# Moved transfers and weight splits around layer one of a fused attention and two-MLP kernel

## The chip, the cores and the metric

One core of a Trainium2 chip. The time is device microseconds of one execution. Engines: PE is TensorE (PEld its weight loads), DVE is VectorE, ACT is ScalarE, POOL is GpSimd, SP is SyncE, which here only issues DMAs. Each engine works off one queue in order.

## The reference, cut to what matters

```python
attn_out = _attn_ref(q, k, v, f)          # causal attention with decay, 4 x 8 heads, 576 x 64
x = attn_out.transpose(0, 2, 1, 3).reshape(2304, 512)
h = x @ moe_w_in; x = (h - tanh(h)) @ moe_w_out              # first MLP, 512 -> 2048 -> 512
h = x @ moe2_w_in; out = (maximum(h, 0) ** 2) @ moe2_w_out   # second MLP
```

The weights reach the kernel as float64: it reads each word as a pair of 32-bit integers and decodes it to float32 itself. All else is float32. The change concerns the second MLP only. "Layer one" below is its first matrix product, "layer two" its second.

## The kernel before, in words

Products are made in float32 accuracy: each operand is split into a high and a low part (fp32r), and each product is three matmuls (high x high, low x high, high x low). The second MLP also uses Strassen-like sums: per tile pair seven products instead of eight, so each weight pair needs seven 256-column pieces: four sums and three plain ones.

**Layer one** (`layer1`, L1185) has 24 units: three token blocks times eight weight pairs p. A step s of the code makes the first four products (6, 1, 7, 5) of unit s and the last three (2, 4, 3) of unit s - 1. Each product (`l1_product`, L1128) is six matmuls of 128x384, and advances a clock (`cw.step`) on which later work is put by a number of products: `cw.later(k, fn)` calls fn k products on. `after1` (L1145) takes a product out of PSUM with ScalarE or VectorE (L1150, L1157, L1167, L1171, L1176) into g tiles, of which there are two buffers for each half of a unit; `store1` (L1179) squares g on GpSimd (L1182) and stores it to DRAM (`gscr`, L1183).

**Weights of layer two** are prepared during layer one. For each of eight pairs: `load_w` (L146) loads the raw words in two halves (L139) into one buffer. `decode_w` (L176) decodes them half by half: ScalarE (`first`, L193 and L194) and VectorE (`bits`, L200 and L202), into `wfull`; the raw buffer serves as scratch for the second half and is free after its L202. `combine` (L232) makes the four sums on GpSimd (L244, into `wsum`) and stores sums (L247) and plain pieces (L249, L250) to a DRAM buffer `wscr`, since layer one's weights still hold the room. `wfull` and `wsum` live in two buffers called `wide`. Decodes follow each other: `decoded()` lets the next begin. In the code `load_w(2, k)` is called at the start of step 4 + 2k and `decode_w(2, k)` at step 5 + 2k (PRE = 5).

When the last token block is through with a weight pair, `final_load` (L307) loads the seven pieces of layer two's pair p from `wscr` into one of two staging buffers (L310), and `final_split` splits them (`split_all`, L287: ScalarE L294 for the high part, VectorE L295 for the low) into the room of layer one's weights. `FREED` (L1225) says at which step of the last block: the load at FREED[p] - 1, the split at FREED[p] + 1.

**Layer two** (`layer2`, L1313) has 36 blocks n. `g_load` (L1232) loads a block of g from `gscr` in four DMAs (L1241), `g_sums` makes three sums on VectorE (L1247, L1248, L1250), `g_split` (L1252) splits it on ScalarE (L1256) and VectorE (L1257) into `gc`, and `l2_product` (L1259) makes seven products of six matmuls of 128x256 (L1270), 42 per block. Block n uses pairs 2q and 2q + 1 with q = n mod 4, so the fourth block is the first to want pairs 6 and 7. Blocks 0 and 1 are loaded during layer one; the rest use buffers `gx` of a pool m3, which is opened over the room of layer one's pool m2 (staging buffers `xl`, g tiles `gt`, split y tiles `T1` to `T7`) when layer one's code ends.

**Order.** The framework puts instructions into each engine's queue by when it reckons their inputs ready, and by the code's order among those that are; `high_priority` moves an instruction forward among these. The order is fixed when the kernel is built, and an engine whose next instruction is not ready waits.

Of the kernel before, what the change touches and what calls it, by code (L numbers as in the profile page):

```python
# [109 lines left out]
def fused_kernel(ctx: ExitStack, tc: tile.TileContext, q, k, v, f, w1i, w1o, w2i, w2o, out):  # L110
# [65 lines left out]
    def decode_w(phase, fc):  # L176
# [20 lines left out]
        def bits(x):  # L197
            lo_, hi_ = spots[x]
            dst = full[:, x * w : (x + 1) * w]
            nc.vector.scalar_tensor_tensor(lo_, in0=hi_, scalar=3, in1=lo_,  # L200
                                           op0=ALU.logical_shift_left, op1=ALU.bitwise_or)
            nc.vector.scalar_tensor_tensor(dst, in0=hi_, scalar=0x80000000, in1=lo_,  # L202
                                           op0=ALU.bitwise_and, op1=ALU.bitwise_or)
            if x == 0:
                first(1)
            else:
                cw.later(LAG['wparts'], (lambda: parts(0)) if phase == 0 else (lambda: combine(phase, fc, full)))

        def parts(x):
# [22 lines left out]
    def combine(phase, p, full):  # L232
        full = full.bitcast(F32)
        (q11, q12), (q21, q22) = quarters(full, phase)
        sums = wide(f"wsum_{phase}_{p}", F32)
        s = [sums[:, 256 * x : 256 * x + 256].rearrange("p (c f) -> p c f", c=2) for x in range(4)]
        if phase == 1:
            ops = ((s[0], q21, q22, ALU.add), (s[1], s[0], q11, ALU.subtract), (s[2], q11, q21, ALU.subtract),
                   (s[3], q12, s[1], ALU.subtract))
        else:  # L240
            ops = ((s[0], q12, q11, ALU.subtract), (s[1], q22, s[0], ALU.subtract), (s[2], q12, q22, ALU.subtract),
                   (s[3], q21, s[1], ALU.subtract))
        for o, a, b, op in ops:
            nc.gpsimd.tensor_tensor(o, in0=a, in1=b, op=op)  # L244
        if phase == 2:
            w = wscr[p]
            nc.sync.dma_start(w[:, 0:4], sums.rearrange("p (k f) -> p k f", k=4))  # L247
            f4 = full.rearrange("p (k f) -> p k f", k=4)
            nc.sync.dma_start(w[:, 4:5], f4[:, 0:1])  # L249
            nc.sync.dma_start(w[:, 5:7], f4[:, 2:4])  # L250
            decoded()
            return
        v = full.rearrange("p (c f) -> p c f", c=ND)
        s4 = sums.rearrange("p (k f) -> p k f", k=4)
        work = split_plan(1, p, (v[:, :, 0:P], v[:, 2:4, P : 2 * P]), [s4[:, 0:2], s4[:, 2:4]])
        split_all(1, p, work, 1)
# [48 lines left out]
    stagew = {}  # L305

    def final_load(p):  # L307
        t = box2["m2"].tile([P, 7, 256], F32, tag="xl", name=f"wst_{p}", bufs=2)
        stagew[p] = t
        nc.sync.dma_start(t, wscr[p])  # L310

    def final_split(p):
        t = stagew.pop(p)
        split_all(2, p, split_plan(2, p, (t[:, 5:7], t[:, 4:5]), [t[:, 0:4]]), 1)

    WHERE = {1: {5: 0, 6: 1, 7: 2, 3: 3, 1: 4, 2: 5, 4: 6}, 2: {5: 0, 6: 1, 7: 2, 4: 3, 2: 4, 3: 5, 1: 6}}

# [861 lines left out]
    def store1(u, fi):  # L1179
        i, p = units1[u]  # L1180
        g = gf.pop((u, fi))
        nc.gpsimd.tensor_tensor(g, in0=g, in1=g, op=ALU.mult)  # L1182
        nc.sync.dma_start(gscr[i][:, :, 2 * p + fi], g.rearrange("p b t n -> p b (t n)"))  # L1183

    def layer1():  # L1185
        n = len(units1)
        last = n - NP2
        for s in range(n + 1):
# [10 lines left out]
                    goal = NF + p + FEED2  # L1199
            if s >= PRE and (s - PRE) % 2 == 0 and (s - PRE) // 2 < NP2:  # L1200
                decode_w(2, (s - PRE) // 2)
            if s >= PRE - 1 and (s - PRE + 1) % 2 == 0 and (s - PRE + 1) // 2 < NP2:
                load_w(2, (s - PRE + 1) // 2)
            if s == n - 3:
                g_load(0)
                g_load(1)
# [9 lines left out]
                cw.step(lambda: l1_product(*x))  # L1216
                feed.pace(goal)
            for p in range(NP2):
                if s == last + FREED[p] - 1:
                    final_load(p)  # L1220
                if s == last + FREED[p] + 1:
                    final_split(p)

    PRE = 5
    FREED = (1, 2, 3, 3, 5, 6, 7, 7)  # L1225
    AT2 = {1: (0, 0), 6: (0, 256), 7: (1, 0), 2: (1, 256), 5: (2, 0), 4: (2, 256), 3: (3, 0)}
    ORDER2 = (1, 6, 7, 2, 5, 4, 3)
    GWHERE = {7: 0, 5: 1, 6: 2, 3: 3, 1: 4, 2: 5, 4: 6}
    graws, gc, r2 = {}, {}, {}
    NG = NBLK * 4  # L1230

    def g_load(n):  # L1232
        j, q = divmod(n, 4)
        if n < 2:
            t = wp.tile([P, 8, 2, P], F32, tag=f"w{15 - n}", name=f"graw_{n}", bufs=1)
        else:
            t = box2["m3"].tile([P, 8, 2, P], F32, tag="gx", name=f"graw_{n}", bufs=2)
        graws[n] = t
        src = gscr[j // 3][:, j % 3, 4 * q : 4 * q + 4].rearrange("p (e i) (h t) -> p i h e t", i=2, h=2)
        for slot, h, i in ((0, 1, 0), (5, 0, 0), (7, 1, 1), (6, 0, 1)):  # L1240
            nc.sync.dma_start(t[:, slot], src[:, i, h])  # L1241

    def g_sums(n):
# [5 lines left out]
                                in0=t[:, 0:2].rearrange("p k e t -> p k (e t)"), in1=both, op=ALU.add)  # L1249
        nc.vector.tensor_tensor(t[:, 4], in0=t[:, 6], in1=t[:, 3], op=ALU.subtract)  # L1250

    def g_split(n):  # L1252
        t = graws.pop(n)
        c = box2["m3"].tile([P, 2, 7, 2, P], F32R, tag="gc", name=f"gc_{n}", bufs=3)
        gc[n] = c
        nc.scalar.activation(c[:, 0], t[:, 1:8], AF.Copy)  # L1256
        nc.vector.tensor_tensor(c[:, 1], in0=t[:, 1:8], in1=c[:, 0].bitcast(F32), op=ALU.subtract)  # L1257

# [54 lines left out]
    def layer2():  # L1313
        m2ctx.close()
        box2["m3"] = ctx.enter_context(tc.tile_pool(name="m3", bufs=1, reuse_waits="tile"))
        with tc.high_priority(offset=L2HOT):
            g_split(0)
        with tc.high_priority(offset=L2HOT // 2):
            g_split(1)
            for n in (2, 3):  # L1320
                g_load(n)
        for n in range(NG):
            for x, k in enumerate(ORDER2):
                if x == 1 and n + 2 < NG:
# [99 lines left out]
```

## Time and profile before

| | us |
|---|---|
| median of three runs (1072.89 to 1077.76) | 1073.69 |
| the profiled execution | 1074.4 |
| its span, first to last instruction | 1072.7 |
| TensorE busy in the span | 1014.9 |
| mean granted TensorE clock | 0.985 of full |

A row of a timeline gives the start, the duration of the merged instructions, the engine, the code line, what it writes and reads, how many, and in square brackets how long the engine stood idle before it and what ended that. Rows of SP are issues of DMAs; their data land later. Matmuls overlap, so that the duration of one is longer than its share of the time.

### The profile page before, as it was taken

Reading aid. Unit: us, or ns where it says so; the run is one execution under the profiler, and the core shown is the slowest. Engines: PE = TensorE matmul, PEld = TensorE weight load, DVE = VectorE, ACT = ScalarE, POOL = GpSimd, SP = SyncE. Lnnn points to the kernel's source line nnn. Section 1 sums busy time; section 2 is a strip of 40 time slices with the busy share of each in tenths; the row PEclk is TensorE's granted clock in tenths of the full one; section 3 lists DMA queues with packets and bytes.
Section 4 is the critical chain, followed back from the end, with each engine's and each line's share of the span. In section 5 each row is a group of like instructions: output and inputs, shape, how many; then the busy total and the mean of one; then the engine's idle time right before and its main releaser. Section 6 shows DMA issues by size and latency. Waiting matters only on the chain. (4 is left out here: it accounts for less than half of the span.)

```text
span 1072.7 us, 20563 instructions
## 1 busy us (share of the span) xinstructions
PE 1014.9 (95%) x7246; PEld 963.7 (90%) x7246; DVE 755.3 (70%) x1596; ACT 587.0 (55%) x1176; POOL 435.5 (41%) x576
## 2 busy tenths in 40 slices
PE   7989999999999999999999999988788869999997
PEld 5779899999999999999998878988688869999997
DVE  5897954777776777777755785766565877778775
ACT  5887854666766666666644664534344553233332
POOL 4763622465455654556411333655655440000000
PEclk9998999999999999999999999999999989999999
DMA  8947642433432333432131235566557763444442
GB/s 228 273 138 236 185 119 72 106 86 80 129 86 70 105 99 90 116 79 73 49 90 59 83 114 169 189 207 210 197 193 236 254 219 110 138 119 137 122 117 79
DMA packets 190903, 146.47 MB, mean 137 GB/s; under 512 B 83568, under 2 KB 168880, under 8 KB 190800
## 3 DMA queue, kind: packets, MB, share of 16 engines
q1 hardware_dynamic: 190752, 145.12, 45.7%
q8 instruction: 57, 0.93, 0.4%
q14 instruction: 46, 0.38, 0.1%
q10 hardware_dynamic: 48, 0.03, 0.0%
HBM read 100.47 MB, written 39.92 MB: 131 GB/s over the span
## 5 line engine op out<-in xcount | busy, mean ns | idle before, releaser
L970 PE MATMUL y<-ghl,w 128*128 128x256 f32 (+1 forms) x1536 | 249.1, 305 | 3.1 <-DVE ghl L951 2.0
L970 PEld LDWEIGHTS y<-ghl,w 128*128 128x128 f32 x1536 | 212.7, 192 | 16.0 <-DVE ghl L951 3.1
L930 PE MATMUL h<-x,w 128*128 128x256 f32 x1344 | 199.8, 290 | 4.9 <-POOL w L216 3.8
L930 PEld LDWEIGHTS h<-x,w 128*128 128x128 f32 x1344 | 174.5, 191 | 9.7 <-POOL w L216 5.0
L1256 ACT ACTIVATE gc<-graw 128x1792 fp32r<-128x1792 f32 x36 | 60.5, 1699 | 117.4 <-DVE graw L1250 107.1
L1138 PE MATMUL r<-yt,ws 128*128 128x384 f32 x576 | 111.0, 340 | 12.9 <-DVE g L1150 12.8
L1138 PEld LDWEIGHTS r<-yt,ws 128*128 128x128 f32 x576 | 100.9, 190 | 18.2 <-DVE g L1150 13.6
L1270 PE MATMUL o<-ws,gc 128*128 128x256 f32 x864 | 117.0, 285 | 0.0
L1270 PEld LDWEIGHTS o<-ws,gc 128*128 128x128 f32 x864 | 110.4, 194 | 0.0
L507 POOL TENSOR_SCALAR Pb<-neg,ccol 128x384 f32<-128x384 f32 (+2 forms) x96 | 69.0, 719 | 91.5 <-PE pt L714 74.0
L621 ACT ACTIVATE Pb<-Pb,st 128x384 f32<-128x384 f32 (+2 forms) x96 | 67.8, 706 | 68.2 <-DVE st L612 68.0
L1182 POOL TENSOR_TENSOR g<-g 128x768 f32<-128x768 f32 x48 | 80.3, 1683 | 54.2 <-ACT g L1171 36.3
L1270 PE MATMUL o<-wq,gc 128*128 128x256 f32 x648 | 92.3, 287 | 10.5 <-ACT gc L1256 8.4
L635 POOL TENSOR_SCALAR Pb<-Pb,st 128x384 f32<-128x384 f32 (+2 forms) x96 | 67.0, 698 | 82.0 <-DVE st L631 49.0
L1138 PE MATMUL r<-yt,wq 128*128 128x384 f32 x432 | 86.6, 343 | 11.9 <-ACT g L1167 9.0
L1270 PEld LDWEIGHTS o<-wq,gc 128*128 128x128 f32 x648 | 84.7, 195 | 11.5 <-ACT gc L1256 8.7
L1138 PEld LDWEIGHTS r<-yt,wq 128*128 128x128 f32 x432 | 76.8, 192 | 15.2 <-ACT g L1167 10.6
L1257 DVE TENSOR_TENSOR gc<-graw,gc 128x1792 fp32r<-128x1792 f32 x36 | 72.1, 2024 | 21.6 <-ACT gc L1256 21.4
L612 DVE CUSTOM_DVE_ANT_0 Pb<-s,Pb 64x288 f32<-64x288 f32 (+2 forms) x160 | 73.9, 476 | 13.6 <-PE s L677 6.9
L943 DVE TENSOR_TENSOR g<-h,g 128x512 f32<-128x512 f32 x72 | 49.5, 687 | 32.7 <-ACT g L940 31.4
L720 DVE TENSOR_TENSOR PT<-pt,PT 128x384 fp32r<-128x384 f32 (+2 forms) x96 | 55.1, 574 | 10.3 <-ACT PT L719 5.6
L951 DVE TENSOR_TENSOR ghl<-g,ghl 128x512 fp32r<-128x512 f32 x72 | 53.8, 747 | 10.2 <-ACT ghl L947 9.9
(148 smaller groups left out, 1874.7 us busy)
## 6 DMA issues: line engine op xcount, KB each, us to landing
gscr<-g SPq DMA_DIRECT2D x48, 384.0 KB, 3.4
graw<-gscr SPq DMA_DIRECT2D x144, 128.0 KB, 2.6
wraw<-in_moe_w_in_dram SPq DMA_DIRECT2D x32, 512.0 KB, 4.6
wraw<-in_moe_w_out_dram SPq DMA_DIRECT2D x32, 512.0 KB, 5.5
neg<-cscr SPq DMA_DIRECT2D x32, 288.0 KB, 3.7
wst<-wscr SPq DMA_DIRECT2D x8, 896.0 KB, 5.4
qk<-in_k_dram SPq DMA_DIRECT2D x48, 128.0 KB, 2.8
v<-in_v_dram SPq DMA_DIRECT2D x48, 128.0 KB, 2.7
```

What stands on the lines that cost most here:

```text
L507: nc.gpsimd.tensor_scalar(pb[:rows, o : o + w], t[:rows, :w], ccol[:rows, ti, b * H + h : b * H + h + 1], 1.0, op0=ALU.add, op1=ALU.mult)
L612: nc.vector.tensor_tensor_reduce(out=d, in0=t[:rows, src : src + m], in1=d, scale=-0.125, scalar=3.0e38 if j == 0 else stat(0, x)[:rows], ...
L621: nc.scalar.activation(d, d, AF.Exp, bias=stat(len(parts) - 1, x)[:rows], scale=-1.0, accum_out=stat(2, x)[:rows])
L635: nc.gpsimd.tensor_scalar(d, d, r, 1.0, op0=ALU.mult, op1=ALU.mult)
L720: cw.later(LAG['trlo'], lambda: nc.vector.tensor_tensor(dst[1], src, dst[0].bitcast(F32), op=ALU.subtract))
L930: nc.tensor.matmul(o, lhsT=win(fc, wh, dc), rhs=xpart(j, dc, xh), start=dc == 0 and wh + xh == 0, stop=dc == ND - 1 and wh == 1)
L970: nc.tensor.matmul(o, lhsT=wout(fc, wh, i * P, P), rhs=ghl[:, xh, fj * n : fj * n + n], start=s == 0 and fj == 0 and wh + xh == 0 and i % ...
L1138: nc.tensor.matmul(t, lhsT=wprod(1, p, k, wh)[:, dc * P : (dc + 1) * P], rhs=yt[i, k][:, xh, dc], start=k in FIRST and dc == 0 and wh + xh ...
L1182: nc.gpsimd.tensor_tensor(g, in0=g, in1=g, op=ALU.mult)
L1256: nc.scalar.activation(c[:, 0], t[:, 1:8], AF.Copy)
L1257: nc.vector.tensor_tensor(c[:, 1], in0=t[:, 1:8], in1=c[:, 0].bitcast(F32), op=ALU.subtract)
L1270: nc.tensor.matmul(o, lhsT=gc[n][:, gh, GWHERE[k], e], rhs=wprod(2, 2 * q + e, k, wh), start=q == 0 and e == 0 and gh + wh == 0 and c0 == ...
```

## The change

1. `bits`: after the last decode step of pair fc of layer two, `load_w(2, fc + 1)` is put one product later. In `layer1` only the first pair is still loaded by step number.
2. `combine`: the two plain stores are put one product later, the store of the sums and `decoded()` five.
3. `store1`: the store of g is put two products later; its squaring stays.
4. `final_load`: pair 6 goes to two tiles of a tag `g` (unused in layer one) and one of m3, pair 7 to the two `wide` buffers, in two DMAs; pairs 0 to 5 as before, at step FREED[p] with a new FREED. Pair 7 is loaded at the step of pair 5, pair 6 at the start of `layer2`.
5. The splits of pairs 6 and 7 are put 2 and 9 products into layer two.
6. `layer2`: the tiles of m3 are allocated in a set order (two `gx`, `st`, a pad, then `gc2`, `gc0`, `gc1` with a tag each), so that `gx` lies over the staging buffers, `gc0` over T6, T1 and T7, and `gc1` over T7, T5 and T3. `g_split(1)` comes behind the loads of blocks 2 and 3.

```diff
--- before.py
+++ after.py
@@ -204,6 +204,8 @@
             if x == 0:
                 first(1)
             else:
+                if phase == 2 and fc + 1 < NP2:
+                    cw.later(1, lambda: load_w(2, fc + 1))
                 cw.later(LAG['wparts'], (lambda: parts(0)) if phase == 0 else (lambda: combine(phase, fc, full)))
 
         def parts(x):
@@ -244,11 +246,17 @@
             nc.gpsimd.tensor_tensor(o, in0=a, in1=b, op=op)
         if phase == 2:
             w = wscr[p]
-            nc.sync.dma_start(w[:, 0:4], sums.rearrange("p (k f) -> p k f", k=4))
             f4 = full.rearrange("p (k f) -> p k f", k=4)
-            nc.sync.dma_start(w[:, 4:5], f4[:, 0:1])
-            nc.sync.dma_start(w[:, 5:7], f4[:, 2:4])
-            decoded()
+
+            def plain():
+                nc.sync.dma_start(w[:, 4:5], f4[:, 0:1])
+                nc.sync.dma_start(w[:, 5:7], f4[:, 2:4])
+
+            def summed():
+                nc.sync.dma_start(w[:, 0:4], sums.rearrange("p (k f) -> p k f", k=4))
+                decoded()
+            cw.later(1, plain)
+            cw.later(5, summed)
             return
         v = full.rearrange("p (c f) -> p c f", c=ND)
         s4 = sums.rearrange("p (k f) -> p k f", k=4)
@@ -305,13 +313,28 @@
     stagew = {}
 
     def final_load(p):
-        t = box2["m2"].tile([P, 7, 256], F32, tag="xl", name=f"wst_{p}", bufs=2)
-        stagew[p] = t
-        nc.sync.dma_start(t, wscr[p])
+        if p == NP2 - 1:
+            s_, r = wide(f"wst_s{p}", F32), wide(f"wst_r{p}", F32)[:, :768]
+            parts = [(s_, 0, 4), (r, 4, 7)]
+        elif p == NP2 - 2:
+            parts = [(m1.tile([P, 512], F32, tag="g", name=f"wst_{x}_{p}", bufs=3), x, x + 2) for x in (0, 2)]
+            r = box2["m3"].tile([P, 3 * 256], F32, tag="st", name=f"wst_r{p}", bufs=1)
+            parts.append((r, 4, 7))
+        else:
+            t = box2["m2"].tile([P, 7 * 256], F32, tag="xl", name=f"wst_{p}", bufs=2)
+            parts = [(t, 0, 7)]
+        views = []
+        for t, a, b in parts:
+            v = t.rearrange("p (k f) -> p k f", f=256)
+            nc.sync.dma_start(v, wscr[p][:, a:b])
+            views.append(v)
+        if len(views) == 1:
+            views = [views[0][:, 0:4], views[0][:, 4:7]]
+        stagew[p] = views
 
     def final_split(p):
-        t = stagew.pop(p)
-        split_all(2, p, split_plan(2, p, (t[:, 5:7], t[:, 4:5]), [t[:, 0:4]]), 1)
+        *s_, r = stagew.pop(p)
+        split_all(2, p, split_plan(2, p, (r[:, 1:3], r[:, 0:1]), s_), 1)
 
     WHERE = {1: {5: 0, 6: 1, 7: 2, 3: 3, 1: 4, 2: 5, 4: 6}, 2: {5: 0, 6: 1, 7: 2, 4: 3, 2: 4, 3: 5, 1: 6}}
 
@@ -1180,7 +1203,7 @@
         i, p = units1[u]
         g = gf.pop((u, fi))
         nc.gpsimd.tensor_tensor(g, in0=g, in1=g, op=ALU.mult)
-        nc.sync.dma_start(gscr[i][:, :, 2 * p + fi], g.rearrange("p b t n -> p b (t n)"))
+        cw.later(2, lambda: nc.sync.dma_start(gscr[i][:, :, 2 * p + fi], g.rearrange("p b t n -> p b (t n)")))
 
     def layer1():
         n = len(units1)
@@ -1199,8 +1222,8 @@
                     goal = NF + p + FEED2
             if s >= PRE and (s - PRE) % 2 == 0 and (s - PRE) // 2 < NP2:
                 decode_w(2, (s - PRE) // 2)
-            if s >= PRE - 1 and (s - PRE + 1) % 2 == 0 and (s - PRE + 1) // 2 < NP2:
-                load_w(2, (s - PRE + 1) // 2)
+            if s == PRE - 1:
+                load_w(2, 0)
             if s == n - 3:
                 g_load(0)
                 g_load(1)
@@ -1216,26 +1239,32 @@
                 cw.step(lambda: l1_product(*x))
                 feed.pace(goal)
             for p in range(NP2):
-                if s == last + FREED[p] - 1:
+                if FREED[p] is None:
+                    continue
+                if s == last + FREED[p]:
                     final_load(p)
-                if s == last + FREED[p] + 1:
+                if s == last + FREED[p] + 1 and p < NP2 - 2:
                     final_split(p)
 
     PRE = 5
-    FREED = (1, 2, 3, 3, 5, 6, 7, 7)
+    FREED = (1, 2, 3, 4, 5, 6, None, 6)
     AT2 = {1: (0, 0), 6: (0, 256), 7: (1, 0), 2: (1, 256), 5: (2, 0), 4: (2, 256), 3: (3, 0)}
     ORDER2 = (1, 6, 7, 2, 5, 4, 3)
     GWHERE = {7: 0, 5: 1, 6: 2, 3: 3, 1: 4, 2: 5, 4: 6}
     graws, gc, r2 = {}, {}, {}
     NG = NBLK * 4
 
-    def g_load(n):
-        j, q = divmod(n, 4)
+    def g_tile(n):
         if n < 2:
             t = wp.tile([P, 8, 2, P], F32, tag=f"w{15 - n}", name=f"graw_{n}", bufs=1)
         else:
             t = box2["m3"].tile([P, 8, 2, P], F32, tag="gx", name=f"graw_{n}", bufs=2)
         graws[n] = t
+        return t
+
+    def g_load(n):
+        j, q = divmod(n, 4)
+        t = graws[n] if n in graws else g_tile(n)
         src = gscr[j // 3][:, j % 3, 4 * q : 4 * q + 4].rearrange("p (e i) (h t) -> p i h e t", i=2, h=2)
         for slot, h, i in ((0, 1, 0), (5, 0, 0), (7, 1, 1), (6, 0, 1)):
             nc.sync.dma_start(t[:, slot], src[:, i, h])
@@ -1249,10 +1278,13 @@
                                 in0=t[:, 0:2].rearrange("p k e t -> p k (e t)"), in1=both, op=ALU.add)
         nc.vector.tensor_tensor(t[:, 4], in0=t[:, 6], in1=t[:, 3], op=ALU.subtract)
 
+    def gc_tile(n):
+        gc[n] = box2["m3"].tile([P, 2, 7, 2, P], F32R, tag=f"gc{n % 3}", name=f"gc_{n}", bufs=1)
+        return gc[n]
+
     def g_split(n):
         t = graws.pop(n)
-        c = box2["m3"].tile([P, 2, 7, 2, P], F32R, tag="gc", name=f"gc_{n}", bufs=3)
-        gc[n] = c
+        c = gc[n] if n in gc else gc_tile(n)
         nc.scalar.activation(c[:, 0], t[:, 1:8], AF.Copy)
         nc.vector.tensor_tensor(c[:, 1], in0=t[:, 1:8], in1=c[:, 0].bitcast(F32), op=ALU.subtract)
 
@@ -1313,12 +1345,21 @@
     def layer2():
         m2ctx.close()
         box2["m3"] = ctx.enter_context(tc.tile_pool(name="m3", bufs=1, reuse_waits="tile"))
+        for x in range(2):
+            g_tile(2 + x)
+        with tc.high_priority(offset=L2HOT):
+            final_load(NP2 - 2)
+        box2["m3"].tile([P, 256], F32, tag="pad", name="pad", bufs=1)
+        for n in (2, 0, 1):
+            gc_tile(n)
         with tc.high_priority(offset=L2HOT):
             g_split(0)
         with tc.high_priority(offset=L2HOT // 2):
-            g_split(1)
             for n in (2, 3):
                 g_load(n)
+            g_split(1)
+        cw.later(2, lambda: final_split(NP2 - 2))
+        cw.later(9, lambda: final_split(NP2 - 1))
         for n in range(NG):
             for x, k in enumerate(ORDER2):
                 if x == 1 and n + 2 < NG:
```

## Rows read from the trace of the kernel before

**Rows 1.** Table by stretches: busy us (instructions) of each engine, granted clock, DMA share, GB/s.
```profile
700.00:818.00 118.00, 98.28 (x522) 92.51 (x522) 73.39 (x105) 51.96 (x91) 71.56 (x57) 0.97 0.62 202
...
870.00:890.00 20.00, 10.95 (x58) 10.36 (x59) 15.38 (x20) 10.71 (x14) 7.64 (x4) 0.74 0.56 177
890.00:910.00 20.00, 20.00 (x169) 20.00 (x168) 16.68 (x24) 7.16 (x5) 0.00 (x0) 1.00 0.44 132
```

**Rows 2.** The chain that ended last, 844 to 880 us: start, us, what.
```profile
844.46 16.95 PE r L1138 x96
```

**Rows 3.** ScalarE's waits, 700 to 818 us: us in total, times, longest.
```profile
ACT wfull L193 <- DMA wraw<-in_moe_w_out_dram: 19.1, 4, 5.5
ACT wraw L193 <- DMA wraw<-in_moe_w_out_dram: 6.8, 2, 4.3
ACT wfull L193 <- issue: 4.9, 1, 4.9
```

**Rows 4.** Timeline of SyncE's queue, 764 to 772 us.
```profile
765.19 0.33 SPq L250 DMA_DIRECT2D wscr<-wfull  x1
767.45 0.33 SPq L247 DMA_DIRECT2D wscr<-wsum  x1
767.88 0.37 SPq L139 DMA_DIRECT2D wraw<-in_moe_w_out_dram  x1
...
770.87 0.62 SPq L139 DMA_DIRECT2D wraw<-in_moe_w_out_dram  x1
```

**Rows 5.** Timeline of all engines, 764 to 775 us.
```profile
764.47 0.69 DVE L202 SCALAR_TENSOR_TENSOR wfull<-wraw 128x512 uint32<-128x512 uint32 x1
...
772.85 0.66 ACT L193 ACTIVATE wfull<-wraw 128x512 uint32<-128x512 uint32 x1 [4.88 <-issue]
...
773.96 0.48 ACT L1167 ACTIVATE g<-r 128x384 f32<-128x384 f32 x1
...
774.49 3.51 PE L1138 MATMUL r<-yt,wq 128*128 128x384 f32 x12 [2.86 <-ACT g L1167]
```

**Rows 6.** Timeline of all engines at the boundary, 871 to 882 us.
```profile
871.84 1.21 PE L1138 MATMUL r<-yt,ws 128*128 128x384 f32 x6
...
879.68 3.29 ACT L1256 ACTIVATE gc<-graw 128x1792 fp32r<-128x1792 f32 x2 [2.83 <-DVE wq L295]
...
881.43 0.80 PE L1270 MATMUL o<-wq,gc 128*128 128x256 f32 x2 [8.39 <-ACT gc L1256]
```

**Rows 7.** Timelines of VectorE and SyncE: the freeing and the load, first and last.
```profile
699.57 0.69 DVE L202 SCALAR_TENSOR_TENSOR wfull<-wraw 128x512 uint32<-128x512 uint32 x1
...
702.97 0.37 SPq L139 DMA_DIRECT2D wraw<-in_moe_w_out_dram  x1
...
779.38 1.84 DVE L202 SCALAR_TENSOR_TENSOR wfull<-wraw 128x512 uint32<-128x512 uint32 x1
...
784.43 1.42 SPq L139 DMA_DIRECT2D wraw<-in_moe_w_out_dram  x2
```

**Rows 8.** DMA issues, 655 to 885 us: count, KB each, median us to landing.
```profile
wraw<-in_moe_w_out_dram SPq DMA_DIRECT2D x16, 512.0 KB, 5.2
...
graw<-gscr SPq DMA_DIRECT2D x16, 128.0 KB, 2.9
```

**Rows 9.** Waits of SyncE's queue and of VectorE, 655 to 885 us.
```profile
SPq L1183 <- POOL g L1182: 98.1, 44, 9.1
...
DVE g L1150 <- DMA gscr<-g: 18.5, 8, 6.4
```

**Rows 10.** Source line L295, 814 to 880 us: duration ns min/median/max, first and last start.
```profile
L295 DVE TENSOR_TENSOR wq<-wst,wq x16: 410/682/1683, 833.1 to 878.0; 128x512 fp32r<-128x512 f32 x8, 128x256 fp32r<-128x256 f32 x8
...
L295 DVE TENSOR_TENSOR ws<-wst,ws x8: 1210/1263/2484, 826.0 to 876.6; 128x1024 fp32r<-128x1024 f32 x8
```

**Rows 11.** Timeline of SyncE's queue at the boundary, 869 to 885 us.
```profile
871.91 8.00 SPq L1183 DMA_DIRECT2D gscr<-g  x4
880.00 4.38 SPq L1241 DMA_DIRECT2D graw<-gscr  x8
```

## The prediction

> **What bounds the kernel now.** I read the table by stretches first. Layer one of the second MLP runs from about 660 to 873 us, layer two after it. The reader should compare matmul counts per microsecond, not busy shares: the busy column looks full where the count is low [rows 1]. What an undisturbed matmul costs comes from the chain of waits: 96 layer-one matmuls in 16.95 us, 0.177 us each [rows 2]. Layer two does 169 in 20 us, 0.118 us each [rows 1]. So:
> - 700 to 818 us holds 522 matmuls, worth 92.2 us: 25.8 us are lost. Idle TensorE is 19.7 us of it, the rest are restarts and a granted clock of 0.97, a little time at 1.2 GHz instead of 2.4.
> - 870 to 890 us: 58 matmuls, 12 of layer one (2.1 us) and 46 of layer two (5.4 us), 7.5 us of work: 12.5 lost, with a granted clock of 0.74 behind the long idle.
>
> Who ended the waits comes next. TensorE waits for ScalarE's and VectorE's reads of its PSUM banks, but these engines are only the messengers. ScalarE's own waits in the first stretch are 19.1 + 6.8 + 4.9 = 30.8 us, in seven pieces, on the decode of weight words (L193) [rows 3]; the one put down to "issue" is followed next and ends with a load too. The timeline shows one such piece: SyncE issues the sums' store L247 at 767.45, the load's first half L139 at 767.88 and its second half only at 770.87 [rows 4]. VectorE's last read of the old words, L202, started at 764.47 and took 0.69, so the buffer was free at 765.16. ScalarE sits 4.88 us before its L193 at 772.85, then gets to the Relu that empties TensorE's PSUM bank (L1167) only at 773.96, and TensorE idles 2.86 us until 774.49 [rows 5]. A wait on ScalarE of some 4.9 us thus costs about 2.9 on TensorE at once: work stored up hides 2 of it.
>
> Last the boundary. Layer one's last matmuls start at 871.84 and take 1.21. ScalarE starts the first split of layer two (L1256) at 879.68, having waited 2.83 us for VectorE's last weight split (L295); TensorE starts at 881.43 after 8.39 us [rows 6].
>
> **The change, part by part.** All sums are against the profiled execution, 1074.4 us; the median shown is 1073.69, 0.7 lower.
>
> *Loads of the decoded weights go out one product after VectorE's last decode step.* Nothing is added or removed: the same 2 issues of SyncE per weight pair, seven times. Code order is not queue order: in the rows the plain store L250 runs ahead of the sums' store L247, which the code calls first [rows 4]. The framework orders each queue by what it takes as ready, and the code's order breaks ties. What changes is the tie: at 765.16 the load is now older than the plain and sums' stores. It can go at once, not 2.7 us later (767.88), and its second half not 5.7 later [rows 4]. There are four such plain cases; the first and the last show the first half issued 2.7 us (700.26 to 702.97) and 3.2 us (781.22 to 784.43) behind the freeing [rows 7]. Since a half lands 5.2 us after issue [rows 8], ScalarE would see its words at about 770.4 instead of 772.85. Both ends: nothing, if ScalarE's decode step is ordered earlier by as much as the load (its place in ScalarE's queue is fixed by the same reckoning); and all lateness, some 3.0 for each of four plain waits, 11.8, and the whole of the other three, 6.8 and one of about 4.8 (19.1 over four): 23.4 of 30.8 us. One us of ScalarE wait costs at most 25.8 / 30.8 = 0.84 us of the stretch, so the ends are 0 and 19.7 us. I take half the plain lateness, 1.5 us in each of seven waits, because the same ordering moves both: 10.5 x 0.84 = 8.8, rounded to 8.5 us.
>
> The Trainium skill, DMA: Bandwidth & Descriptors, section "Anatomy of one DMA", gives a fit of 2.0 us plus bytes over 436 GB/s (for DMAs issued by GpSimd), an estimated 3.2 us for this load. The trace disagrees: 5.2 us for SyncE's loads, and the measurement decides; by the page's price the waits would shrink by 2 us more each, and the sum would be that of the most favourable rival below.
>
> *The plain and sums' stores move behind.* Same three issues. Queued behind a waiting L247 were the load and g stores; now the load no longer is. Who needs the stores: the buffer of the next decoded words. Cost nothing: these stores are out within 3 us of the load while the load itself takes 5.2. If that cover goes, ScalarE waits for a store instead (rival 2).
>
> *g stores move two products back.* SyncE waits 98.1 us in 44 pieces for GpSimd before them [rows 9], so in code two products later (12 matmuls, 2.1 us) most should still go when GpSimd is done. VectorE waits 18.5 us for stores to land, so a real delay is not free (rival 4). Taken as zero; lower bound in the rival.
>
> *Loads of summed weights one step later, two taken out of the rotation.* Pairs 0 to 5 still alternate in two buffers and each load still follows the split that frees its buffer: zero for these. Pair 7 gets the decode's scratch, free by then, in two pieces; pair 6 is loaded at the boundary in three. Three issues more, 0.4 to 0.6 us each like L139's [rows 4], on a queue that nobody waits for there unless rival 3 holds.
>
> *Layer two's buffers are laid out anew, and the splits of pairs 6 and 7 follow the first products.* Today the first split waits for the last staging buffer; then it lies over y tiles whose last readers are an earlier step's products, so it can run before layer one ends. That takes the 12.5 us away: nothing else on the path to 881.43 is late, and the code does the first block's sums a step before. What is late next is VectorE. In layer two it works 16.68 us beside 169 matmuls [rows 1], 4.15 us for a block of 42, which TensorE does in 4.97. Pairs 6 and 7 are wanted by the fourth block, 14.9 us in. Until then VectorE has three blocks' work, 12.4 us, and now both weight splits, 1.26 + 0.68 + 0.41 each by the medians and, for the smallest piece, the minimum [rows 10]: 12.4 + 4.7 = 17.1 us in 14.9, 2.2 too much if nothing was done ahead. Ends: 0, as the first block's work falls into layer one, and 4.7 if both splits lie open; I take 2.0, the row's own balance. Net of the boundary: 10.5 us.
>
> **Sum:** 8.5 + 10.5 = 19.0 off 1074.4 is 1055.4; less 0.7, **1054.7 us** for the median.
>
> **The rivals.**
> 1. *Forecast*, both parts: 1054.7, own range 1047 to 1060.
> 2. *Only the boundary counts.* ScalarE's decode step moves up with the load, or waits for the plain store instead; waits stay near 4.9. For it: four plain waits are so alike that their place looks set by one reckoning of the load's length. Against: half the lateness is SyncE's queueing. 1073.69 - 10.5 = 1063.2.
> 3. *The boundary stall moves into layer two and the loads gain nothing*, so that the change does not do what it says. Today SyncE issues the third block's loads (L1241) at 880.00, behind the last four g stores, 7 us after layer one's last product (873.0) [rows 6, 11]. Kept so, they land 2.9 us later [rows 8], at 882.9; ScalarE's half of the split, 1.65 (two in 3.29 [rows 6]), and VectorE's 4.15 follow: 888.7, while layer two, starting at 873.0, wants the block two blocks on, at 882.9. Price 5.8, and 12.5 - 5.8 - 2.0 = 4.7 gain: 1069.0. For it: the four stores hold the queue for 8.00 us [rows 11]. Against it: the loads' new buffers are those of weight pairs 4 and 5, free before the last stores are due.
> 4. *Slower: g stores really leave 2.1 us later* and VectorE's adds wait for their two-deep buffers. Place: L1150 behind the landing of a store, 8 times now [rows 9]. Price per store 2.1 x 0.84 = 1.8 us; six stores eat the boundary's 10.5, from nine on the kernel is slower by over 0.5% (5.4 us, about what a measurement of this kernel can tell from no change). Twelve of 48: 1073.69 + 21.6 - 10.5 = 1084.8. For: there is no third buffer. Against: SyncE already waits at 44 of 48.
> 5. *All lateness goes and VectorE fits:* 12.5 + 19.7 = 32.2, 1041.5. For it: all of it is there to be had. Against: the ordering that moves with the loads, and VectorE's balance above. The price of the Trainium skill's DMA: Bandwidth & Descriptors, "Anatomy of one DMA", would end here; the rows do not bear it out, and it adds nothing to this rival's chance.
>
> **How the numbers follow.** Chances: forecast 0.50, rival 2 0.22, rival 3 0.11, rival 4 0.08, rival 5 0.09. Faster by over 0.5% (below 1068.3) are the forecast, rivals 2 and 5: 0.81. Rival 3 lies within 0.5%: 0.11. Slower: 0.08. The range 1043 to 1069 leaves out rival 4, half of rival 3 above it and half of rival 5 below it, about 0.18.
>
> **What would show it.** Right: ScalarE's waits on weight loads in layer one fall from 30.8 us to about 20, the 118 us of 700 to 818 hold some 50 matmuls more, the first half of a load follows L202 within 1 us; TensorE passes from layer one to two with under 1 us idle and a clock of 1.0 there; L295 of pairs 6 and 7 stands after the first layer-two matmul. Wrong: ScalarE's waits at L193 as long as before; an idle TensorE before the third or fourth block; longer waits of L1150 for stores of g.

## The result and the profile after

| | us |
|---|---|
| median before, beside it (4 runs) | 1074.70 |
| median after (4 runs, 1063.42 to 1066.06) | 1064.35 |
| ratio, 95% interval | 0.9903 [0.9875, 0.9931] |
| the profiled execution after, its span | 1064.87, 1063.2 |

The kernel is 10.4 us faster, not the 19.0 of the forecast. Where the time went is read by stages, from the starts and ends of the two layers' matmuls in the two profiled executions:

| us | before | after | gained |
|---|---|---|---|
| start to first matmul of layer one | 660.3 | 658.9 | 1.4 |
| layer one | 212.7 | 202.0 | 10.7 |
| idle between the layers | 8.4 | 7.3 | 1.1 |
| first matmul of layer two to the end | 191.3 | 195.0 | -3.7 |

The first row is scatter: in the kernels below, whose engines do the same work in the same order up to there, layer one starts between 655.7 and 666.3 us. In these two executions layer one gained somewhat more than its 8.5 us; the boundary and layer two together, forecast at 10.5, lost 2.6. The table by stretches of the changed kernel shows both (columns as in [rows 1]):

```profile
700.00:818.00 118.00, 104.30 (x579) 99.83 (x580) 77.73 (x111) 55.80 (x97) 78.08 (x60) 1.00 0.71 235
860.00:870.00 10.00, 2.73 (x14) 2.38 (x12) 9.10 (x8) 7.87 (x11) 7.43 (x4) 0.74 0.35 119
960.00:1060.00 100.00, 96.02 (x782) 95.20 (x780) 72.50 (x105) 32.90 (x23) 0.00 (x0) 0.98 0.38 111
```

In 700 to 818 us there are 579 matmuls for 522 [rows 1], 57 x 0.177 = 10.1 us of work. Part of layer one's 10.7 us is the clock. Over layer one's own stretch, before and after, TensorE idles 212.73 - 187.84 = 24.9 us and 202.03 - 183.77 = 18.3, and the granted clock is 0.98 and 1.00:

```profile
660.31:873.04 212.73, 187.84 (x1021) 178.69 (x1019) 139.82 (x202) 97.29 (x171) 119.27 (x90) 0.98 0.66 214
658.89:860.92 202.03, 183.77 (x1021) 175.99 (x1019) 137.60 (x200) 95.03 (x169) 119.13 (x89) 1.00 0.69 223
```

The same program in another execution (e8 below) took 205.4 us there, with 19.1 us idle at a clock of 0.98. The boundary's hole is still there, only earlier. And layer two, which should be plain sailing, does 782 matmuls from 960 to 1060 us; before it did 814 in the same window:

```profile
960.00:1060.00 100.00, 97.89 (x814) 97.48 (x814) 76.90 (x110) 34.26 (x24) 0.00 (x0) 1.00 0.42 122
```

**Layer one, closer.** VectorE's last read of the old words (now from 755.93, for 1.84 us), then SyncE's queue of the changed kernel:

```profile
755.93 1.84 DVE L202 SCALAR_TENSOR_TENSOR wfull<-wraw 128x512 uint32<-128x512 uint32 x1
```
```profile
757.87 0.57 SPq L252 DMA_DIRECT2D wscr<-wfull  x1
758.54 1.02 SPq L139 DMA_DIRECT2D wraw<-in_moe_w_out_dram  x2
759.61 0.45 SPq L253 DMA_DIRECT2D wscr<-wfull  x1
```

Words free at 757.77, load issued at 758.54 and both halves at once: 0.77 us, for 2.7 and 5.7 in [rows 4]. That is the longest of the changed kernel's seven loads of this kind: their first halves leave 0.07 to 0.77 us behind the freeing, and three of the second halves 2.1 to 4.3 us behind it. So ScalarE no longer waits for the load in this stretch, but for the store of the plain pieces, which keeps the `wide` buffer (ScalarE's waits after, 700 to 818 us; us in total, times, longest):

```profile
ACT wfull L193 <- DMA wscr<-wfull: 6.9, 2, 3.9
ACT wfull L193 <- issue: 4.3, 1, 4.3
```

11.2 us for 30.8 [rows 3]. The wait put down to "issue" is counted with them.

**The boundary, closer.** Timeline of all engines of the changed kernel:

```profile
859.72 1.21 PE L1161 MATMUL r<-yt,ws 128*128 128x384 f32 x6
...
860.39 3.47 DVE L303 TENSOR_TENSOR ws<-wst,ws 128x512 fp32r<-128x512 f32 x2 [0.50 <-ACT ws L302]
...
865.11 1.04 ACT L302 ACTIVATE ws<-wst_s 128x1024 fp32r<-128x1024 f32 x1
...
866.18 1.95 DVE L303 TENSOR_TENSOR ws<-wst_s,ws 128x1024 fp32r<-128x1024 f32 x1 [0.46 <-ACT ws L302]
866.47 3.27 ACT L1288 ACTIVATE gc<-graw 128x1792 fp32r<-128x1792 f32 x2
868.18 5.09 DVE L1289 TENSOR_TENSOR gc<-graw,gc 128x1792 fp32r<-128x1792 f32 x2
868.20 0.79 PE L1302 MATMUL o<-wq,gc 128*128 128x256 f32 x2 [7.27 <-ACT gc L1288]
...
870.71 2.67 SPq L1270 DMA_DIRECT2D graw<-gscr  x5
871.39 1.23 PE L1302 MATMUL o<-wq,gc 128*128 128x256 f32 x4 [1.11 <-DVE gc L1289]
```

The splits of pairs 6 and 7 (L302 and L303, tiles `wst` and `wst_s`) come later in the code than layer two's first split (L1288), but before it in both queues: ScalarE's starts at 866.47, 5.5 us after layer one's last product (860.92).

**Layer two, closer.** One of the places where the changed kernel stalls:

```profile
982.34 1.70 ACT L1288 ACTIVATE gc<-graw 128x1792 fp32r<-128x1792 f32 x1 [5.34 <-DVE graw L1279]
...
984.48 4.00 DVE L1289 TENSOR_TENSOR gc<-graw,gc 128x1792 fp32r<-128x1792 f32 x2
984.73 1.70 ACT L1288 ACTIVATE gc<-graw 128x1792 fp32r<-128x1792 f32 x1 [0.69 <-DVE graw L1279]
986.53 3.96 SPq L1270 DMA_DIRECT2D graw<-gscr  x8
...
986.56 0.74 PE L1302 MATMUL o<-wq,gc 128*128 128x256 f32 x4 [1.84 <-DVE gc L1289]
```

This is a ring. The next loads (L1270) leave at 986.53 because only then has VectorE's split (L1289) let a `gx` buffer go; there are two. The data land, VectorE sums them, ScalarE waits 5.34 us for these sums, then splits; VectorE splits; the buffer is free for the load after next. From the ends of VectorE's splits (blocks 2 to 35) the ring needs 5.11 us a block before and 5.15 after, while TensorE does an undisturbed block in 5.04. So the splits' lead over TensorE (the end of a block's split to the block's first matmul) wears away: in blocks 1 to 9 it swings from 2.8 to 6.1 us before and from 1.0 to 4.6 after, and TensorE waits once it is used up, at blocks 32 and 34 before, from block 18 on after. Of the 3.7 us that layer two lost, 0.8 is in its first block (8.97 us for 8.19) and 2.8 in these blocks. A TensorE that starts earlier only spends this lead sooner. None of this stood in the sum of the prediction.

### The profile page after: what moved, and what is told of

Its sections match the earlier page's. It is cut to its first block, busy times and chain, and to the rows that moved or that the text cites. A ratio compares the mean times of both kernels' runs of the same rounds, so it can differ in the third digit from the quotient of the medians.

```text
span 1063.2 us, 20566 instructions
## 1 busy us (share of the span) xinstructions
PE 1010.9 (95%) x7246; PEld 961.1 (90%) x7246; DVE 757.1 (71%) x1597; ACT 585.7 (55%) x1177; POOL 435.6 (41%) x576
## 4 chain that ended last, share of the span: by engine, by line
PE 59%; DMA 7%; DVE 7%; issue 4%; POOL 4%; ACT 3%; SPq 2%; DVEq 0%; ACTq 0%; POOLq 0%
PE y L993 15%; PE h L953 15%; PE o L1302 13%; PE pt L737 4%; PE pv L808 3%; PE r L1161 3%; DMA wscr<-wfull 2%; POOL g L1205 2%; PE s L699 2%; PE s L700 2%; DVE gc L1289 1%; POOL wsum L246 1%; DMA gscr<-g 1%; DVE wfull L202 1%; DMA graw<-gscr 1%
## 5 line engine op out<-in xcount | busy, mean ns | idle before, releaser
L1288 ACT ACTIVATE gc<-graw 128x1792 fp32r<-128x1792 f32 x36 | 60.6, 1699 | 112.9 <-DVE graw L1279 92.7
L1205 POOL TENSOR_TENSOR g<-g 128x768 f32<-128x768 f32 x48 | 81.1, 1704 | 48.1 <-ACT g L1194 38.7
L1289 DVE TENSOR_TENSOR gc<-graw,gc 128x1792 fp32r<-128x1792 f32 x36 | 73.2, 2054 | 15.8 <-ACT gc L1288 15.8
L246 POOL TENSOR_TENSOR wsum<-wfull 128x256 f32<-128x256 f32 x32 | 28.2, 882 | 84.1 <-DVE wfull L202 72.4
```

## The experiments

A median is compared with the kernel before that ran beside it, on the same chip.

| run | edit | ratio to before, 95% interval | layer one, us | idle, us | layer two to the end, us |
|---|---|---|---|---|---|
| the change | | 0.9903 [0.9875, 0.9931] | 202.0 | 7.3 | 195.0 |
| e1_queues_only | parts 1 to 3 | 0.9916 [0.9890, 0.9942] | 205.6 | 8.8 | 190.8 |
| e2_boundary_only | parts 4 to 6 | 1.0024 [1.0005, 1.0042] | 213.5 | 7.3 | 196.1 |
| e3_load_only | part 1 | 0.9939 [0.9915, 0.9964] | 204.9 | 9.4 | 194.7 |
| e4_split_pool | change, first split freed | 0.9946 [0.9927, 0.9965] | 202.4 | 0.5 | 204.3 |
| e5_before4 | before, four g buffers | 0.9947 [0.9929, 0.9965] | 213.3 | 9.1 | 188.3 |
| e6_after4 | change, four g buffers | 0.9860 [0.9842, 0.9877] | 205.7 | 7.3 | 190.2 |
| e7_early4 | e4 and four g buffers | 0.9794 [0.9773, 0.9815] | 204.3 | none | 188.6 |
| e8_plain_now | change, plain stores at once | 0.9921 [0.9892, 0.9949] | 205.4 | 5.5 | 194.1 |
| e9_plain_first | before, plain stores first | 0.9995 [0.9980, 1.0010] | 212.7 | 8.6 | 192.7 |
| e10_plain_hot | change, plain stores hurried | 0.9906 [0.9888, 0.9923] | 204.5 | 6.9 | 196.0 |
| e11_early4_hot | e7 and e10 | 0.9809 [0.9790, 0.9827] | 204.5 | none | 189.2 |

The last three columns come from each run's profiled execution.

### One half of the change at a time

e1 is the kernel before with parts 1 to 3 alone, e2 with parts 4 to 6 alone, e3 with part 1 alone, as the diff ahead has them.

> Parts 1 to 3 alone (load one product after the last decode step, stores of the decoded weights and of g later); staging, splits and layer two's buffers as before. Theory (the whole gain is layer one's; the boundary part brings nothing and costs some 4 us in layer two): 1060 to 1065 us, ScalarE's waits at the decode (L193) near the changed kernel's, an idle TensorE of 6 to 9 us at the boundary. Rival (the staging part makes a good share of layer one's gain, by freeing SyncE and ScalarE in the last token block): 1067 us or more.

> Parts 4 to 6 alone: staging of pairs 6 and 7, later splits, layer two's buffers laid out anew; loads and stores of layer one as before. Theory: 1072 to 1078 us, no gain, decode waits about 31 us, and still some 7 us of idle TensorE at the boundary. Rival (boundary part is worth the 10 us forecast for it, and something in layer one hides it when both are made): 1063 to 1068 us.

> Part 1 alone: the load goes out one product after the last decode step, all stores where they were. Theory (SyncE's wait for the sums' store ahead of the load was the cost): 1062 to 1067 us, decode waits 10 to 18 us. Rival (ScalarE's decode step moves up with the load and only the moved stores give it room): 1070 us or more, decode waits above 22 us.

Of the three theories' ranges only e2's was met (1077.10 us). e1's 1067.90 lies in its rival's range and e3's 1069.36 between its two, as do its waits on the decode, 19.7 us; the kernel before beside them, 1076.01, was 1.3 us above the one beside the change. By the ratios e1 cannot be told from the whole change, so the parts of layer one bring its gain within the intervals. The parts of the boundary alone (e2) cost 1.1 us by the medians and 2.6 by the ratio, 0.0024 of 1076. In the profiles they take 1.1 us off the idle and add 4.8 to what follows. The load alone brings most of layer one's gain; the 1.5 us between e3 and e1 lie inside the intervals.

### Freeing layer two's first split

The room of the split's target lies in the pool m3, opened over the pool m2, and m3's room counts as free only when the last tile of m2 has gone: a g tile, squared and stored late. In e4 m2 is two pools, and layer two's buffers lie in two pools over them, so that `gc0` no longer waits for g tiles (excerpts):

```diff
+        box2["m2b"] = m2bctx.enter_context(tc.tile_pool(name="m2b", bufs=1, side="right"))
...
-        yt[i, k] = box2["m2"].tile([P, 2, 2, NU1], F32R, tag=f"T{k}", name=f"yt_{i}_{k}", bufs=1)
+        yt[i, k] = box2["m2b" if k in SECOND else "m2"].tile([P, 2, 2, NU1], F32R, tag=f"T{k}", name=f"yt_{i}_{k}", bufs=1)
...
-            gf[u, 1] = box2["m2"].tile([P, 3, 2, P], F32, tag="gt", name=f"g1_{u}", bufs=2)
+            gf[u, 1] = box2["m2b"].tile([P, 3, 2, P], F32, tag="gt", name=f"g1_{u}", bufs=2)
...
+        box2["m3b"] = ctx.enter_context(tc.tile_pool(name="m3b", bufs=1, reuse_waits="tile", side="right"))
```

> The changed kernel, with layer one's pool of y tiles, staging and g tiles cut in two: staging and the y tiles of the first four products in one, g tiles and the y tiles of the last three in another, and layer two's buffers over them likewise, so that the first block's split buffer no longer belongs to a pool that opens only when layer one's last g tile is stored. Theory (the pool's opening set the place of the first split in the queues of ScalarE and VectorE): idle TensorE at the boundary below 2 us, 1055 to 1060 us. Rival (VectorE's work is what is late there: two weight splits and the last adds): the idle time stays at 5 us or more or comes back before the second to fourth block, 1062 to 1066 us.

TensorE now passes over with half a microsecond idle, as the theory had it, and yet the kernel is slower than the changed one, 0.9946 for 0.9903: its 1070.20 us lies above both ranges. TensorE's timeline, a window of layer two, and TensorE's waits from 860 to 1065 us, all of e4:

```profile
863.94 0.50 PE L1303 MATMUL o<-wq,gc 128*128 128x256 f32 x2 [0.54 <-ACT gc L1289]
866.00 0.74 PE L1303 MATMUL o<-wq,gc 128*128 128x256 f32 x4 [1.55 <-DVE gc L1290]
```
```profile
960.00:1040.00 80.00, 75.24 (x606) 72.78 (x605) 55.84 (x79) 26.76 (x18) 0.00 (x0) 1.00 0.41 121
```
```profile
PE o L1303 <- DVE gc L1290: 10.5, 13, 1.8
```

The 7 us went again in many small waits for VectorE's split. The lead is never above 1.7 us here, and the ring needs 5.50 us a block; why it is slower than the 5.15 of the change was not tried.

### Four buffers for g

To test the ring, blocks of g go through four buffers in turn: the two that blocks 0 and 1 used are taken again. In e5 (before), e6 (change) and e7 (e4):

```diff
-        if n < 2:
-            t = wp.tile([P, 8, 2, P], F32, tag=f"w{15 - n}", name=f"graw_{n}", bufs=1)
+        if n % 4 < 2:
+            t = wp.tile([P, 8, 2, P], F32, tag=f"w{15 - n % 4}", name=f"graw_{n}", bufs=1)
```

> The kernel before, with one thing changed: layer two's g blocks are loaded into four buffers in turn in place of two. Theory (layer two is bound by its feed: a g block's load can't be issued until the split of two blocks earlier has let its buffer go, and the chain load, sums, splits takes 5.11 us a block against TensorE's 5.04): the lead of the splits no longer shrinks, the waits of 0.5 and 2.1 us inside layer two go, and the kernel takes 1070 to 1074 us against some 1076 before. Rival (VectorE's own work sets the pace of the feed, the buffers don't): the lead shrinks as before and the time stays within 1 us.

> The changed kernel, with g blocks loaded into four buffers in turn. Theory (feed through two buffers): the longer blocks of layer two (8.97, 6.29, 8.62, 5.59 us where an undisturbed one takes 5.04) mostly go, layer two lasts about 187 us from its first matmul in place of 191, and the kernel takes 1058 to 1062 us. Rival (VectorE's work sets the pace): those blocks stay, 1063 to 1066.

> The changed kernel with its last pool of layer one cut in two (so that layer two's first split no longer queues behind the weight splits; boundary idle 0.5 us) and g blocks in four buffers. Theory (the early start was only lent, because the feed through two buffers could not keep up): blocks of layer two come back to about 5.04 us and the boundary's 7 us are at last kept, 1050 to 1058 us. Rival (VectorE's work sets the pace): blocks stay at 5.2 to 5.5 us and the time at 1064 to 1071, as with two buffers.

The times fit the theory in e5 and e7. e6's 1062.99 us lies 1 us above its theory's range, just under its rival's; its long blocks did go, but for the first, which took 9.66 us, so that layer two lasted 190.2 us and not 187. One thing is not parted by these runs: with four buffers the framework also builds another order for VectorE, which sums a block of g earlier among the splits. ScalarE's largest group of waits in layer two, 890 to 1060 us, turns round: before (first fence), its split waited for the sums of g; in e5 (second) it waits for TensorE to be done with an older block, so that TensorE sets the pace. The third fence is e5's window of [rows 1]'s table.

```profile
ACT gc L1256 <- DVE graw L1250: 101.9, 22, 6.8
```
```profile
ACT gc L1256 <- PE o L1270: 80.0, 24, 3.3
```
```profile
960.00:1060.00 100.00, 100.00 (x836) 100.00 (x835) 73.37 (x105) 34.73 (x24) 0.00 (x0) 1.00 0.38 112
```

Of e5, and of e6 too, no block but the first and the last takes longer than 5.04 us. The four buffers, with that order, are worth 1077.31 - 1072.05 = 5.3 us to the kernel before, and 1068.62 - 1062.99 = 5.6 to the changed one (e8, below, is the same program as the change, and ran beside e6). To the kernel with the freed split they are worth most: 0.9946 falls to 0.9794. Here at last the boundary pays: e7 is 1062.99 - 1056.40 = 6.6 us below e6, whose split is not freed. Timeline of e7, and its window:

```profile
863.29 1.68 ACT L1289 ACTIVATE gc<-graw 128x1792 fp32r<-128x1792 f32 x1
...
866.27 0.40 PE L1303 MATMUL o<-wq,gc 128*128 128x256 f32 x2
...
867.26 0.62 ACT L302 ACTIVATE ws<-wst 128x512 fp32r<-128x512 f32 x1
...
879.33 1.01 PE L1303 MATMUL o<-wq,gc 128*128 128x256 f32 x3 [1.77 <-DVE gc L1290]
```
```profile
960.00:1040.00 80.00, 80.00 (x674) 80.00 (x673) 60.67 (x86) 29.13 (x20) 0.00 (x0) 1.00 0.39 113
```

The first split runs beside layer one's last products, TensorE passes over without a gap, and the weight splits follow. Two waits are left, 0.42 us in the first block and 1.77 at 879.33, in the third. At 1056.40 us this kernel beats the one before and the changed one.

The Trainium skill, Trainium Kernel Development and Optimization, section "Best Practices", says to double-buffer so that DMA and compute overlap. The trace agrees that two buffers overlap them, and shows that here two are not enough: from the ends of VectorE's splits, 5.11 us a block with two and, the lead growing back, 4.90 with four (e5), for a consumer that takes 5.04.

### Which store, and when

e8 is the changed kernel with `plain()` in place of `cw.later(1, plain)`.

> The changed kernel, with the stores of the plain halves issued as soon as the decode has written them, in place of two products later; all else as changed. Theory (after the change ScalarE's decode waits for the plain store to let the wide buffer go, 11.2 us in 3 waits): these waits shrink to under 5 us, and the time is 1059 to 1064 us. Rival (SyncE then waits for the decode before it can issue the loads, as before the change): the waits move back to the loads, and the time is 1064 to 1068.

Neither came true. The framework built the same instructions in the same order, with the same waits, on every engine: the code's point of issue lies within what the reckoned readiness decides anyway. So e8 is a second measurement of the change: 0.9921, and its layer one took 205.4 us, not 202.0. The changed kernel built without part 1 (built only, not run) has the very same order too, and without part 3 one g store and one group of layer-one loads change places. Built the other way, part 3 alone changes nothing in the kernel before, and part 2 alone gives it e1's order but for that g store. So part 2 already moves the load, part 1 alone (e3) builds another order that moves it too, and part 3 is next to nothing.

e9 undoes nothing and delays nothing; in the kernel before, the stores of `combine` stand in the order plain, plain, sums, which changes SyncE's order alone.

> The kernel before, with one thing changed: the two stores of the plain halves stand ahead of the store of the sums in the code; nothing is issued later, the loads and the g stores stay where they were. On every engine but SyncE the instructions come in the order of the kernel before; on SyncE the stores change places. Theory (layer one's gain comes from the loads that SyncE issues ahead of the stores, so the stores' own order is worth nothing): 1074 to 1078 us beside some 1076 before, ScalarE's waits for the load stay near 31 us. Rival (it is the plain stores, which let the wide buffer go, that had to come earlier, and the move of the load is not needed): 1066 to 1071 us.

The theory's range held: the stores' order by itself is worth nothing. ScalarE's waits on L193, 700 to 818 us, stay, at 30.1 us in the three rows:

```profile
ACT wfull L193 <- issue: 13.2, 3, 5.9
ACT wfull L193 <- DMA wraw<-in_moe_w_out_dram: 9.6, 2, 4.9
ACT wraw L193 <- DMA wraw<-in_moe_w_out_dram: 7.3, 2, 4.7
```

e10 and e11 issue the second plain store right behind the first, in the change and in e7:

```diff
             def plain():
-                nc.sync.dma_start(w[:, 4:5], f4[:, 0:1])
-                nc.sync.dma_start(w[:, 5:7], f4[:, 2:4])
+                with tc.high_priority(offset=L2HOT):
+                    nc.sync.dma_start(w[:, 4:5], f4[:, 0:1])
+                    nc.sync.dma_start(w[:, 5:7], f4[:, 2:4])
```

> The changed kernel, with its two stores of plain halves given priority, so that SyncE issues the second right behind the first and not behind loads and g stores. Theory (what is left of ScalarE's waiting in layer one is for these stores, which let the wide buffer go: 11.2 us in 3 waits, one of them of 4.3 us behind a second store that SyncE issued 5 us after the first could be written): the waits fall to under 6 us and layer one (from its first matmul to its last) takes 196 to 201 us in place of 202; 1059 to 1064 us. Rival (the loads then come later by the stores' 0.6 us each and the wait goes back to the load, or g stores and sums come late): 1064 to 1070 us.

> The kernel with the pool cut in two and g blocks in four buffers (1056.4 us), with the plain stores given priority as in e10. Theory (layer one's rest is a wait for these stores): 1051 to 1056 us. Rival (the wait only changes its name): 1056 to 1061 us.

e10's rival came true: the wait goes back to the load and the time stays. e11's 1055.83 us lies in its theory's range by 0.2, but its ratio, 0.9809 for e7's 0.9794, shows no gain, which tells nothing apart. But e10 shows something that neither theory had. ScalarE's waits on L193 and TensorE's waits, 700 to 818 us, in e10:

```profile
ACT wfull L193 <- DMA wraw<-in_moe_w_out_dram: 13.9, 4, 5.3
ACT wraw L193 <- DMA wraw<-in_moe_w_out_dram: 11.0, 4, 5.5
ACT wfull L193 <- POOL wsum L246: 2.9, 1, 2.9
ACT wfull L193 <- issue: 1.5, 1, 1.5
```
```profile
PE r L1162 <- ACT yt L1106: 5.1, 2, 4.0
PE r L1162 <- DVE yt L1107: 4.6, 3, 2.4
PE r L1162 <- DVE g L1174: 2.3, 1, 2.3
PE r L1162 <- ACT g L1191: 1.7, 3, 0.7
```

ScalarE waits 29.3 us there, nearly as long as before the change (30.8), and TensorE waits 13.7, for 19.5 before in the same view. In e3 it is 19.7 us of ScalarE's waits (17.2 for the sums' store) and 12.1 of TensorE's. Layer one takes 202.0 to 205.7 us in every kernel whose engines' orders changed with parts 1 or 2, whichever DMA ScalarE waits for, and 212.7 to 213.5 in all four that have neither (before, e2, e5 and e9, which has the swap of stores alone). TensorE idles 14.9 to 19.8 us of it in the first nine, at granted clocks of 0.96 to 1.00, and 23.6 to 24.9 in the four, at 0.98.

## Why the prediction was right, and where it was wrong

**The sign and the range held**; the value, 1054.7, is 9.7 us low. Of the two terms one came, by a working that the runs refute, and the other did not come at all; that the sum stayed inside a range of 26 us is in good part luck.

**The layer-one term, 8.5 us: right in size, not by its working.** Over the nine profiled kernels with the new order layer one takes 204.4 us on average, over the four with the old 213.1: 8.7 us. Right were the load within 1 us of L202 (0.77) and some 50 matmuls more (57). The step that failed is the price, "One us of ScalarE wait costs at most 25.8 / 30.8 = 0.84 us of the stretch". ScalarE's waits fell to 11.2, not to about 20; by that price, (30.8 - 11.2) x 0.84, the gain would have been 16.5; the measured 8.7 makes 0.44. But in e10 the waits fell by 1.5 us alone, 30.8 to 29.3, and the gain was there, far over "at most". So a wait of ScalarE has no fixed price here; that its price is set by what stands behind it in the queue is likely, but not shown. That the new order is worth some 8.7 us is shown; which exchange in SyncE's, ScalarE's, VectorE's or GpSimd's queue carries it is open, since none of these edits moved one engine's order alone save e9, whose swap on SyncE was worth nothing.

**The stores at zero: right**, though their cover did go, as rival 2 had it: ScalarE waits for the plain store, which SyncE issues behind the loads. e10 put that right and nothing came of it. The g stores at zero: right; rival 4 has no support (VectorE's waits for them to land went from 18.5 [rows 9] to 22.8 us, and the kernel got faster).

**The boundary term, 10.5 us: wrong.** The step is "That takes the 12.5 us away: nothing else on the path to 881.43 is late". It failed twice. First, the split did not come first: "it can run before layer one ends" took the code's order and the room's last readers for enough, and left out that the new pool's room waits for the old pool's last tile. Idle fell from 8.39 to 7.27 us. Second, and worse, the path went on past 881.43. The prediction asked whether VectorE's work for a block fits into TensorE's time for it, 4.15 us in 4.97, and took the fit for no wait; the ring of load, sums and splits through two buffers has its own period, 5.11 us, and a lead that an early start uses up. e4 shows that the first fault mended alone gives nothing; e7 that both together give some 16 us more, 0.9946 to 0.9794 of 1076 (by the medians 1070.20 to 1056.40, 14 us). The 2.0 us for VectorE's crowding was aimed at the fourth block; e7's one long wait is in the third, 1.77 us.

**The rivals.** Rival 2's 1063.2 is nearest and its reason the wrong way round: the loads counted, the boundary did not. Rival 3 had right that the loads of g still leave behind the last g stores, at 870.71, 9.8 us after layer one's last product at 860.92, and that layer two would stall; but its third block had its split 1.1 us ahead in the changed kernel and did not wait, and only where layer two starts early, in e4 and e7, is there a wait of 1.77 us in that block. What happened is the forecast's loads and nothing from the boundary, 1073.69 - 8.5 = 1065.2; no rival held that pair.

## What to carry to other kernels

Ask of a stage behind a gap not only whether each engine has time enough, but what period its ring of buffers has, and how the producer's lead runs over the stage: where the lead shrinks, closing the gap in front gives nothing until the ring is mended. Before costing an edit that moves an issue in the code, look at the order the queues get: three edits here gave orders that were the same, or all but the same, without them. And a wait on an engine beside the bottleneck has no fixed price: ask what stands behind it in its queue.

## What the hardware showed that was not expected

Equal stalls of TensorE cost unequally. Before, 1.89 us idle in layer two's block 34 made it 7.18 us long, 2.1 more than 5.04, at a granted clock of 1.00 (first row). After, 1.84 us idle at 986.56 made block 22 8.62 us long, 3.6 more, as the windows behind it show (the other rows): the clock fell to half, 1.2 GHz. Mean clocks of 0.93, 0.50 and 0.71 over 2 us each make 3.4 us at half speed, 1.7 us lost. Why the one stall cost clock and the other did not is not shown.

```profile
1058.00:1060.00 2.00, 1.30 (x11) 1.30 (x12) 2.00 (x2) 0.56 (x1) 0.00 (x0) 1.00 0.00 0
986.00:988.00 2.00, 1.44 (x11) 1.45 (x12) 2.00 (x2) 0.42 (x1) 0.00 (x0) 0.93 0.16 44
988.00:990.00 2.00, 2.00 (x11) 2.00 (x11) 0.91 (x2) 0.00 (x0) 0.00 (x0) 0.50 0.83 233
990.00:992.00 2.00, 2.00 (x15) 2.00 (x14) 1.33 (x3) 0.47 (x1) 0.00 (x0) 0.71 0.82 236
```

VectorE's weight splits beside GpSimd took far longer than their medians: two of 128x512 took 3.47 us at 860.39 (1.59 and 1.95 singly), where the median of one such is 0.693 (by code line, the changed kernel):

```profile
L303 DVE TENSOR_TENSOR ws<-wsum,ws x16: 678/693/1720, 592.1 to 696.7; 128x512 fp32r<-128x512 f32 x16
```

GpSimd squared g (L1205) from 859.97 for 3.34 us, in two instructions that end at 861.44 and 863.31; each of VectorE's two, which started 0.4 to 0.5 us behind one of these, ended 0.54 us after it. The Trainium skill, SBUF — State Buffer, section "SBUF: two separate sides", says that VectorE, where it has two inputs in SBUF, and a GpSimd operation that reads SBUF take a shared pair of ports as an exclusive lock, whichever starts first keeping it for its whole instruction. The trace agrees with that, but no run here took GpSimd's work away.
